# Six gathered tiles of a routed-expert kernel transposed by VectorE in quarter rows instead of by TensorE; joint gate inserts, a later table load, and another order of the last three units

## The chip, the cores and the metric

The kernel runs on one core of a Trainium2 chip. The metric is device time in microseconds, of the whole program, as the median of several executions. Besides, one execution was profiled; all rows below are from it. Its engines: TensorE (PE; PEld is its weight load), VectorE (DVE), ScalarE (ACT), GpSimd (POOL) and SyncE (SP), which issues plain DMAs in the order of its program. GpSimd issues the indirect DMAs (gathers and scatters).

## The reference

Three layers follow each other, all in float32:

```python
# 1. attention in chunks of 64: q, k, v are (4, 8, 576, 64)
scores = np.matmul(q_c, k_c.transpose(0, 1, 2, 4, 3)) / np.sqrt(D)
attn = softmax(scores)                  # per chunk
x = np.matmul(attn, v_c)                # -> (2304, 512)
# 2. dense layer: w_in (512, 2048), w_out (2048, 512)
h = x @ w_in
x = (h * np.clip(h + 3.0, 0.0, 6.0) / 6.0) @ w_out
# 3. routed experts: 8 experts, w1 (8, 512, 1024), w2 (8, 1024, 512)
noisy = x @ w_gate + np.log1p(np.exp(x @ w_noise)) * noise
top2 = the two largest of the 8 logits of each token
top2_w = softmax of these two
for e in range(8):
    for k in range(2):
        mask = top2[:, k] == e
        h = np.maximum(x[mask] @ w1[e], 0.0)
        out[mask] += top2_w[mask, k, None] * (h @ w2[e])
```

## The kernel before

Tokens are 18 tiles of 128. Every float32 matrix product is made from three passes (`PASSES`) of a high and a low part of each operand, so each tensor that TensorE reads is first split: ScalarE writes the high part, VectorE the low part.

The dense layer runs in five blocks of 4, 3, 4, 4 and 3 tiles; a block loops over 16 units of 128 hidden columns. In a unit TensorE computes the first layer (`mlp_s1`, L316, 12 matmuls), ScalarE and VectorE make the activation and its split (L357, L358, L362, L370), and TensorE adds the second layer of the unit before (`mlp_o`, L328, 3 matmuls for each tile). From the last block on, each unit also takes one unit of expert weights in (`pump`: L135 loads 512 KB, L141 and L142 split them); the raw loads have three buffers, and the load for three units ahead is issued behind L142.

The experts run in ten groups of rows: expert 0 in two (`(0, 0)` with 3 tiles, `(0, 1)` with 2), experts 1 to 6 in one of 5 tiles (608 rows), expert 7 in two again. A group loops over 8 units (`exp_h`: L316, L634, L635; `exp_o`: L328). Its rows come by a table: `gate_pos` gives every token a slot, and GpSimd writes the token's number and weight there (L557, two writes for a tile of tokens). `exp_slots` loads the table of a group (L568). Then there are two ways to bring rows in:

- `exp_gather` gathers whole rows of a tile by one indirect DMA (L609), and `exp_tr` transposes them by four TensorE transposes (L619), after which ScalarE and VectorE split them out of PSUM (L622, L623).
- `exp_slots_q`, `exp_index` and `exp_gather_q` make row numbers of quarter rows (L578, L580: SyncE; L586: VectorE), gather by four indirect DMAs for each tile (L592), and `exp_tr_q` transposes by VectorE in blocks of 32 x 32 (L407) and splits (L604, L605).

Before, groups (0, 0), (0, 1) and (1, 0) go the first way, all later ones the second. The order of TensorE, VectorE and ScalarE is the order of the program's text, from the last block on that of SyncE too; GpSimd's order is the scheduler's. Work put in between hangs on two clocks: `side`, a list run at the end of a unit, and `ticks`, run inside matmul sequences, where `tick()` counts 4 matmuls of a first layer or 3 of a second. `route` puts the gate of one block's tokens on ticks: `gate_t` transposes a tile (L431, L434), `gate_m` makes its logits (L447, L452), `gate_r` turns them back (L460, L469), `gate_top` picks two experts (L488 to L522, in four parts), and `gate_pos` (L534, L535 on TensorE, L550 to L557) gives the slots.

The gate of block 3 runs in block 4, that of block 4 in group (0, 0). At the end, `exp_last` does the last two units tile by tile, and `exp_y` scales a finished tile by its weights (L659, L661) and has GpSimd add it to the output (L662).

## Time and profile before

| what | us |
|---|---|
| median of 3 runs (lowest to highest) | 930.3 (928.49 to 930.64) |
| the profiled execution | 939.06 |
| its span, from the first to the last instruction | 937.2 |
| TensorE busy in the span | 909.9 (97%) |
| last MLP block and its gate | 388.8 to 471.6 |
| group (0, 0) | 471.6 to 513.8 |
| group (0, 1) | 513.8 to 536.6 |

A row of a timeline gives the start, the duration, the engine, the line, the operation with its tiles, and how many instructions were merged. A bracket at its end is the idle time of the engine before it and what ended it. SPq is SyncE issuing DMAs. TensorE's ends are modelled, so rows that follow each other overlap by some tenths: the distance from start to start is what counts.

### The profile page before, as it was taken

How to read it: one execution, taken by the hardware profiler on the slowest of the kernel's cores; microseconds unless marked ns; L12 is line 12 of the kernel's file. 1: busy time of each engine (PE TensorE's matmuls, PEld its weight loads, DVE VectorE, ACT ScalarE, POOL GpSimd, SP SyncE). 2: the span in 40 equal slices, each digit the busy share in tenths (PEclk: the TensorE clock that was granted, in tenths of full speed). 3: DMA queues.
4: the chain of work that ended last, by engine and by line, in shares of the span. 5: the costliest groups of instructions: out<-in, count | busy, mean ns of one | idle time of the engine just before them, and what ended most of it. 6: DMA issues, size and time to landing. Idle time of an engine off the chain costs nothing. (4 is left out here: it accounts for less than half of the span.)

```text
span 937.2 us, 14383 instructions
## 1 busy us (share of the span) xinstructions
PE 909.9 (97%) x5804; PEld 771.1 (82%) x5804; DVE 480.7 (51%) x908; ACT 330.7 (35%) x637; POOL 229.4 (24%) x213
## 2 busy tenths in 40 slices
PE   7999999999999999998999998999999999999996
PEld 4777788877778778877888887888898989888885
DVE  7999956545543553354552545444545444441311
ACT  4555633323322332243531533333433333321210
POOL 1000000030002000304005263663655445332311
PEclk9999999999999999999999998999999999999998
DMA  9736522121257400033532762563637355240422
GB/s 341 231 106 196 165 76 83 64 54 53 69 197 249 113 5 0 17 97 102 158 102 54 175 145 87 118 153 109 148 103 154 93 124 136 69 55 20 54 24 33
DMA packets 49916, 101.49 MB, mean 108 GB/s; under 512 B 17040, under 2 KB 23056, under 8 KB 49840
## 3 DMA queue, kind: packets, MB, share of 16 engines
q1 hardware_dynamic: 38736, 80.38, 27.4%
q0 software_dynamic: 11104, 20.10, 11.8%
q8 instruction: 47, 0.77, 0.4%
q14 instruction: 29, 0.24, 0.1%
HBM read 77.66 MB, written 22.75 MB: 107 GB/s over the span
## 5 line engine op out<-in xcount | busy, mean ns | idle before, releaser
L328 PE MATMUL bp<-w,g 128*128 128x512 f32 (+1 forms) x1812 | 454.5, 397 | 5.4 <-ACT g L362 3.2
L328 PEld LDWEIGHTS bp<-w,g 128*128 128x128 f32 (+1 forms) x1812 | 330.1, 186 | 81.5 <-ACT g L362 4.6
L316 PE MATMUL bp<-Xa,w 128*128 128x304 f32 (+3 forms) x1344 | 241.6, 330 | 2.9 <-ACT Xa L294 1.3
L316 PEld LDWEIGHTS bp<-Xa,w 128*128 128x128 f32 x1344 | 210.4, 189 | 26.3 <-issue 2.5
L557 POOL DMA_INDIRECT table<-pay,slot x36 | 36.0, 999 | 439.9 <-DVE slot L554 430.5
L592 POOL DMA_INDIRECT xrq<-x2d,iq x114 | 118.0, 1035 | 101.8 <-DVE iq L586 40.7
L635 DVE SCALAR_TENSOR_TENSOR g<-bp,g 128x304 fp32r<-128x304 f32 (+2 forms) x128 | 60.0, 472 | 144.2 <-ACT g L634 123.2
L142 DVE TENSOR_TENSOR w<-raw,w 128x1024 fp32r<-128x1024 f32 x64 | 78.5, 1226 | 90.1 <-ACT w L141 64.4
L634 ACT ACTIVATE g<-bp 128x304 fp32r<-128x304 f32 (+2 forms) x128 | 54.1, 425 | 181.0 <-PE bp L316 149.3
L316 PE MATMUL bp<-Xe,w 128*128 128x304 f32 (+1 forms) x672 | 106.4, 313 | 2.9 <-issue 2.7
L316 PEld LDWEIGHTS bp<-Xe,w 128*128 128x128 f32 x672 | 102.5, 192 | 7.3 <-issue 4.2
L316 PE MATMUL bp<-Xb,w 128*128 128x384 f32 (+1 forms) x480 | 106.3, 365 | 0.0
L316 PEld LDWEIGHTS bp<-Xb,w 128*128 128x128 f32 x480 | 86.1, 188 | 11.7 <-issue 1.0
L662 POOL DMA_INDIRECT out_dram<-arena,tab x40 | 63.1, 1577 | 125.6 <-DVE arena L659 102.2
L358 DVE SCALAR_TENSOR_TENSOR r<-r,bp 128x512 f32<-128x512 f32 (+1 forms) x80 | 50.6, 633 | 83.0 <-ACT r L357 73.6
L141 ACT ACTIVATE w<-raw 128x1024 fp32r<-128x1024 f32 x64 | 67.7, 1058 | 60.6 <-PE bp L328 42.6
L357 ACT ACTIVATE r<-bp,b 128x512 f32<-128x512 f32 (+1 forms) x80 | 51.3, 641 | 105.0 <-PE bp L316 102.2
L370 DVE TENSOR_TENSOR g<-r,g 128x512 fp32r<-128x512 f32 (+1 forms) x80 | 51.0, 637 | 39.7 <-ACT g L362 38.3
L362 ACT ACTIVATE g<-r 128x512 fp32r<-128x512 f32 (+1 forms) x80 | 47.3, 591 | 51.4 <-DVE r L358 47.2
L190 ACT ACTIVATE w<-u 128x512 fp32r<-128x512 f32 x32 | 20.3, 634 | 36.6 <-DVE u L177 33.9
L407 DVE STREAM_TRANSPOSE arena<-xrq 128x512 f32<-128x512 f32 (+1 forms) x30 | 31.3, 1044 | 0.0
L197 DVE TENSOR_TENSOR w<-u,w 128x512 fp32r<-128x512 f32 x32 | 22.0, 688 | 1.4
(152 smaller groups left out, 455.7 us busy)
## 6 DMA issues: line engine op xcount, KB each, us to landing
raw<-in_w2u_dram SPq DMA_DIRECT2D x64, 512.0 KB
raw<-in_w1u_dram SPq DMA_DIRECT2D x24, 512.0 KB
arena<-in_qkv_dram SPq DMA_DIRECT2D x14, 768.0 KB
out_dram<-zero SPq DMA_DIRECT2D x4, 1536.0 KB
rawx<-in_w1u_dram SPq DMA_DIRECT2D x8, 512.0 KB
x2d<-x SPq DMA_DIRECT2D x15, 256.0 KB
xq<-x2d SPq DMA_DIRECT2D x44, 64.0 KB
xrq<-x2d,iq POOLq DMA_INDIRECT x114
```

What stands on the lines that cost most here:

```text
L141: nc.scalar.activation(w[:, 0], raw, AF.Copy)
L142: nc.vector.tensor_tensor(w[:, 1], raw, w[:, 0].bitcast(F32), op=ALU.subtract)
L316: nc.tensor.matmul(dst, w[:, a, kd * P:(kd + 1) * P], x[:, b, kd, t0:t0 + n], start=(k == 0), stop=(k == 3 * KD - 1))
L328: nc.tensor.matmul(acc[i][:gi.shape[2]], gi[:, a], w[:, b, DM:], start=(first and j == 0), stop=(last and j == 2))
L357: nc.scalar.activation(r, st["h", b], AF.Relu, bias=b3)
L358: nc.vector.scalar_tensor_tensor(r, r, 6.0, st["h", b], op0=ALU.min, op1=ALU.mult)
L362: nc.scalar.activation(st["g", b, u][:, 0], st["r", b], AF.Copy)
L370: nc.vector.tensor_tensor(g[:, 1], st["r", b], g[:, 0].bitcast(F32), op=ALU.subtract)
L592: nc.gpsimd.indirect_dma_start(out=xr[:, c * P:(c + 1) * P], out_offset=None, in_=x2q, in_offset=bass.IndirectOffsetOnAxis(ap=st["iq", key ...
L634: nc.scalar.activation(g[:, 0, t0:t0 + n], h, AF.Relu)
L635: nc.vector.scalar_tensor_tensor(g[:, 1, t0:t0 + n], h, 0.0, g[:, 0, t0:t0 + n].bitcast(F32), op0=ALU.max, op1=ALU.subtract)
L662: s = nc.gpsimd.indirect_dma_start(out=out, out_offset=bass.IndirectOffsetOnAxis(ap=tab[:n, i, 0:1], axis=0), in_=y, in_offset=None, compu ...
```

## The change

Five things are changed.

- Groups (0, 0) and tiles 0 to 2 of group (1, 0) are brought in by quarter rows: `exp_slots_q`, `exp_index`, `exp_gather_q` and `exp_tr_q` take the place of `exp_slots`, `exp_gather` and `exp_tr`. For group (0, 0) the turns move from units 11 to 13 to units 12 to 14. Tiles 3 and 4 of group (1, 0) keep the first way, but their transposes move to units 1 and 2 of group (0, 1), and the others come in units 3, 5 and 6; indices and first gathers are put ahead of the second layer that ends group (0, 0).
- `route` handles two tiles (of four) or three (of three) at once: transposes of all, then one `gate_m`, one `gate_r`, with a third tile `at2` for the copies. `gate_top` has other ticks, and `gate_pos` moves from tick 26 to 24 in block 4 and from 17 to 13 in group (0, 0).
- In block 4 the table is loaded 18 ticks after `gate_pos`, and index and gathers follow 12 ticks later; in group (0, 0) they stay with `gate_pos`.
- `exp_last` does the last three units tile by tile (the second layer of unit 5 is left out of its old place); the activation of unit 7 has its own buffer.
- The last tile's scaling is split in halves between VectorE and ScalarE.

```diff
--- before.py
+++ after.py
@@ -95,7 +95,7 @@
     early = const.tile([P, NE], F32, name="early")
     quarter = const.tile([P, 1], F32, name="quarter")
     wg_sb = const.tile([P, KD, 32], F32, name="wg_sb")
-    lp = const.tile([P, 2 * P], F32, name="lp")
+    lp = const.tile([P, 3 * P], F32, name="lp")
     noise_sb = const.tile([P, NTILE, NE], F32, name="noise_sb")
     pay = const.tile([P, NTILE, 2, 2], I32, name="pay")
     cnt = const.tile([P, NE + 1], I32, name="cnt")
@@ -431,14 +431,15 @@
             nc.tensor.transpose(pt[:, kd, :], x, ident)
 
     def gate_cp(t, i=1):
-        nc.scalar.activation(at_[i], st.pop(("x2p", t)), AF.Copy)
-        st["x2T", t] = at_[i].rearrange("p b (c j) -> p b c j", c=KD)
+        x = at_[i] if i < 2 else work.tile([P, KD, P], F32, tag="r", bufs=2, name="at2")
+        nc.scalar.activation(x, st.pop(("x2p", t)), AF.Copy)
+        st["x2T", t] = x.rearrange("p b (c j) -> p b c j", c=KD)
 
     ENDS = [pairs[0][:, :2 * P], pairs[0][:, 6 * P:]]
 
-    def gate_m(t, tag="p6"):
-        gate_mm([t], bank(tag, [P, P], "lg"))
-        gate_lp([t])
+    def gate_m(ts, tag):
+        gate_mm(ts, bank(tag, [P, DM], "lg"))
+        gate_lp(ts)
 
     def gate_mm(ts, lg):
         for i, t in enumerate(ts):
@@ -451,9 +452,9 @@
     def gate_lp(ts):
         nc.scalar.activation(lp[:, :len(ts) * P], st.pop(("lg", ts[0])), AF.Copy)
 
-    def gate_r(t, tag="p6"):
-        gate_rt([t], bank(tag, [P, P], "lt"))
-        gate_rr([t])
+    def gate_r(ts, tag):
+        gate_rt(ts, bank(tag, [P, DM], "lt"))
+        gate_rr(ts)
 
     def gate_rt(ts, lt):
         for i in range(len(ts)):
@@ -586,11 +587,11 @@
         nc.vector.tensor_scalar(iq[:, :tq.shape[1]], tq, float(KD), quarter, op0=ALU.mult, op1=ALU.add)
         st["iq", key] = iq
 
-    def exp_gather_q(key, i):
+    def exp_gather_q(key, i, rows=NROW):
         xr = work.tile([P, DM], F32, tag="x2", bufs=3, name="xrq")
         for c in range(min(P, st["xg", key].shape[3] - i * P) // 32):
             nc.gpsimd.indirect_dma_start(
-                out=xr[:, c * P:(c + 1) * P], out_offset=None, in_=x2q,
+                out=xr[:, c * P:(c + 1) * P], out_offset=None, in_=x2q[:rows * KD],
                 in_offset=bass.IndirectOffsetOnAxis(ap=st["iq", key][:, i * KD + c:i * KD + c + 1], axis=0))
         st["xr", key, i] = xr
 
@@ -625,8 +626,11 @@
     def exp_h(key, e, u, nt):
         x, w = st["xg", key], st["w", e, u]
         n = x.shape[3]
-        g = gtile()[:, :2 * n].rearrange("p (j n) -> p j n", j=2)
-        st["g", key, u] = g
+        if (key, u) == ((NE - 1, 1), U2 - 1):
+            g = work.tile([P, DM], F32R, tag="r", bufs=2, name="gl")
+        else:
+            g = gtile()
+        g = st["g", key, u] = g[:, :2 * n].rearrange("p (j n) -> p j n", j=2)
         parts = [(0, n)] if n <= DM else [(0, n // 2), (n // 2, n // 2)]
         for t0, n in parts:
             h = hbank(n)
@@ -637,7 +641,7 @@
 
     def exp_last(key, e, nt):
         for i in range(nt):
-            for u in (U2 - 2, U2 - 1):
+            for u in range(U2 - 3, U2):
                 g, w = tile_of(st["g", key, u], i), st["w", e, u]
                 for j, (a, b) in enumerate(PASSES):
                     nc.tensor.matmul(st["acc", key][i][:g.shape[2]], g[:, a], w[:, b, DM:],
@@ -655,7 +659,10 @@
             n = min(P, rows - i * P)
             y, acc = arena[:n, i], st["acc", key][i][:n]
             sc = tab[:n, i, 1:2].bitcast(F32)
-            if i % 2 == 0 or key == (NE - 1, 1):
+            if (key, i) == ((NE - 1, 1), nt - 1):
+                nc.vector.tensor_scalar(y[:, :DM // 2], acc[:, :DM // 2], sc, None, op0=ALU.mult)
+                nc.scalar.activation(y[:, DM // 2:], acc[:, DM // 2:], AF.Copy, scale=sc)
+            elif i % 2 == 0 or key == (NE - 1, 1):
                 nc.vector.tensor_scalar(y, acc, sc, None, op0=ALU.mult)
             else:
                 nc.scalar.activation(y, acc, AF.Copy, scale=sc)
@@ -818,7 +825,7 @@
         for f, *a in lst:
             f(*a)
 
-    EU = 11
+    EU = 12
     prev = []
 
 
@@ -981,22 +988,28 @@
 
     groups += [((NE - 1, 0), NE - 1, 0, 3, ("b", 0)), ((NE - 1, 1), NE - 1, 3, CT - 3, ("a", 0))]
 
-    def route(g, grp, rows, n0=17, late=0):
+    def route(g, grp, rows, n0=13, late=0, settle=0):
 
         t, nt = GRP[g]
-        steps = []
-        for i in range(nt):
-            steps += [(5 + 2 * i, gate_r, t + i, "p" + "76"[i % 2]), (3 + 2 * i, gate_m, t + i, "p" + "76"[i % 2]),
-                      (2 if i == 1 else 1 + 2 * i, gate_t, t + i, "p6" if i == 1 else "p5", i % 2)]
-        steps.sort(key=lambda x: (x[0], (gate_r, gate_t, gate_m).index(x[1])))
-        steps = [(n + late, *a) for n, *a in steps]
-        last = 3 + 2 * nt + late
-        d = (n0 - last) // 4
+        steps, n = [], late
+        for k in (3,) if nt == 3 else (2, 2):
+            ts = list(range(t, t + k))
+            steps += [(n + 1 + i, gate_t, t + i, ("p5", "p6", "p7")[i], i) for i in range(k)]
+            steps += [(n + k + 2, gate_m, ts, "p5" if k == 3 else "p7"), (n + k + 4, gate_r, ts, "p6" if k == 3 else "p7")]
+            t, n = t + k, n + k + 3
+        last = n + 2
+        d = max((n0 - last) // 4, 1)
         steps += [(last + i * d, gate_top, g, 1) for i in range(4)]
         if g == len(GRP) - 1:
             steps += [(last, gate_base, g)]
-        steps += [(n0, gate_pos, g), (n0, exp_slots, *grp)]
-        steps += [(n0, exp_gather, grp[0], i, rows) for i in range(grp[3])]
+        steps.sort(key=lambda x: x[0])
+        steps += [(n0, gate_pos, g)]
+        if settle:
+            steps += [(n0 + settle, exp_slots_q, *grp), (n0 + settle + 12, exp_index, grp[0])]
+            steps += [(n0 + settle + 12, exp_gather_q, grp[0], i, rows) for i in range(grp[3])]
+        else:
+            steps += [(n0, exp_slots, *grp)]
+            steps += [(n0, exp_gather, grp[0], i, rows) for i in range(grp[3])]
         for n, f, *a in steps:
             at(ticks, st["tick"] + n, f, *a)
 
@@ -1016,9 +1029,9 @@
     order = tc.manual_schedule(engines={nc.tensor.engine, nc.vector.engine, nc.scalar.engine, nc.sync.engine})
     order.__enter__()
     side = {}
-    at(side, 0, route, len(GRP) - 2, groups[0], NROW - BT[NB - 1] * P, 26, 3)
+    at(side, 0, route, len(GRP) - 2, groups[0], NROW - BT[NB - 1] * P, 24, 3, 18)
     for i in range(3):
-        at(side, EU + i, exp_tr, (0, 0), i)
+        at(side, EU + i, exp_tr_q, (0, 0), i)
     regular(NB - 1, side)
 
 
@@ -1029,10 +1042,12 @@
         if gi == 0:
             at(side, 5, counts)
         elif gi == 1:
-            at(side, 0, exp_slots, *nxt_)
-            for i in range(nxt_[3]):
-                at(side, i, exp_gather, nxt_[0], i)
-                at(side, min(3 + i, 7), exp_tr, nxt_[0], i)
+            for i in (3, 4):
+                at(side, i - 2, exp_tr, nxt_[0], i)
+            for i in range(3):
+                if i:
+                    at(side, i, exp_gather_q, nxt_[0], i)
+                at(side, (3, 5, 6)[i], exp_tr_q, nxt_[0], i)
             at(side, 4, exp_slots_q, *after)
         elif gi == 2:
             at(side, 0, exp_index, nxt_[0])
@@ -1061,6 +1076,11 @@
                     at(side, (3, 5, 6)[i], exp_gather_q, after[0], i)
         for u in range(U2):
             if (gi, u) == (1, 0):
+                exp_slots_q(*nxt_)
+                exp_index(nxt_[0])
+                for i in (3, 4):
+                    exp_gather(nxt_[0], i)
+                exp_gather_q(nxt_[0], 0)
                 exp_o(prevg[0], prevg[1], U2 - 1, prevg[2])
                 exp_y(*prevg)
             exp_h(key, e, u, nt)
@@ -1071,7 +1091,8 @@
                 exp_last(key, e, nt)
                 st["most"] = nc.values_load(cnt[0:1, NE:], min_val=0, max_val=RGN)
             elif u > 0:
-                exp_o(key, e, u - 1, nt)
+                if (gi, u) != (len(groups) - 1, U2 - 2):
+                    exp_o(key, e, u - 1, nt)
             elif prevg is None:
                 for b, v in prev:
                     mlp_o(b, v)
```

## Rows read from the trace of the kernel before

**Rows 1.** First part of the page: busy time and share of each engine.

```profile
PE 909.9 (97%) x5804; PEld 771.1 (82%) x5804; DVE 480.7 (51%) x908; ACT 330.7 (35%) x637; POOL 229.4 (24%) x213
```

**Rows 2.** Timeline around the first wait of TensorE.

```profile
436.90 0.38 SPq L568 DMA_DIRECT2D tab<-table  x1
...
441.98 1.06 ACT L141 ACTIVATE w<-raw 128x1024 fp32r<-128x1024 f32 x1 [6.03 <-DMA raw<-in_w2u_dram]
...
445.37 3.91 PE L328 MATMUL bp<-w,g 128*128 128x512 f32 x9 [2.87 <-ACT g L362]
```

**Rows 3.** Stretches: length, PE busy (matmuls), granted clock, DMA share, GB/s.

```profile
445.40:449.10 3.70, 3.70 (x9) 0.54 0.94 269
...
510.54:514.00 3.46, 3.46 (x19) 1.00 0.64 182
```

**Rows 4.** Chain of waits, group (0, 1): start, us, what.

```profile
522.14 1.41 PE bp L328 x6
523.55 0.47 PE bp L619 x4
524.01 1.33 PE bp L316 x12
```

**Rows 5.** Timeline of TensorE at its second wait.

```profile
510.54 0.75 PE L619 MATMUL bp<-ident,xr 128*128 128x128 f32 x4 [1.23 <-DMA xr<-x2d,tab]
```

**Rows 6.** Timeline of TensorE at its third wait.

```profile
562.41 0.46 PE L328 MATMUL bp<-w,g 128*96 128x512 f32 x1 [0.57 <-issue]
...
565.60 7.14 PE L316 MATMUL bp<-Xe,w 128*128 128x304 f32 x24 [2.74 <-issue]
```

**Rows 7.** Timeline of units of the last MLP block.

```profile
427.67 2.26 PE L316 MATMUL bp<-Xa,w 128*128 128x384 f32 x12
...
431.86 2.25 PE L316 MATMUL bp<-Xa,w 128*128 128x384 f32 x12
...
460.61 2.27 PE L328 MATMUL bp<-w,g 128*128 128x512 f32 x9
...
460.87 0.58 ACT L357 ACTIVATE r<-bp,b 128x384 f32<-128x384 f32 x1 [1.09 <-PE bp L316]
...
462.08 0.53 ACT L362 ACTIVATE g<-r 128x384 fp32r<-128x384 f32 x1 [0.62 <-DVE r L358]
...
462.92 1.06 ACT L141 ACTIVATE w<-raw 128x1024 fp32r<-128x1024 f32 x1 [0.32 <-PE bp L328]
...
464.01 1.23 DVE L142 TENSOR_TENSOR w<-raw,w 128x1024 fp32r<-128x1024 f32 x1 [0.82 <-ACT w L141]
```

**Rows 8.** Timeline of SyncE, table and row numbers in group (0, 1).

```profile
527.26 0.43 SPq L568 DMA_DIRECT2D tab<-table  x1
...
532.39 1.88 SPq L580 DMA_DIRECT2D tq<-tq  x3
```

**Rows 9.** DMA traffic, 40 slices of 0.1 us from 558.5.

```profile
GB/s 0 41 0 0 0 0 0 0 0 82 246 82 164 41 41 0 0 0 0 0 0 0 246 123 246 41 0 0 0 164 164 0 0 287 41 123 205 246 328 369
```

**Rows 10.** Timeline of the end.

```profile
927.81 1.56 POOL L662 DMA_INDIRECT out_dram<-arena,tab  x1 [15.26 <-DVE arena L659]
...
929.68 1.43 POOL L662 DMA_INDIRECT out_dram<-arena,tab  x1 [0.31 <-issue]
```

**Rows 11.** Timeline of the gate in group (0, 0).

```profile
485.42 0.27 PE L460 MATMUL bp<-ident,lp 128*128 128x128 f32 x1
...
490.11 0.56 DVE L510 TENSOR_TENSOR macc<-macc,m 128x8 bf16<-128x8 bf16 x3
```

**Rows 12.** Timeline of one tile turned by VectorE in group (1, 0).

```profile
569.70 1.10 DVE L407 STREAM_TRANSPOSE arena<-xrq 128x512 f32<-128x512 f32 x1
...
571.49 0.69 DVE L605 TENSOR_TENSOR Xa<-arena,Xa 128x512 fp32r<-128x512 f32 x1 [0.70 <-ACT Xa L604]
```

**Rows 13.** Timeline of GpSimd.

```profile
516.26 1.57 POOL L662 DMA_INDIRECT out_dram<-arena,tab  x1 [0.30 <-DVE g L635]
...
559.08 0.94 POOL L592 DMA_INDIRECT xrq<-x2d,iq  x1 [0.30 <-issue]
```

## The prediction

> **What bounds the kernel now.** First the share of each engine on the page: TensorE is busy for 97% of the span [rows 1], so time can be won only by taking work from it or by closing its gaps. So the next view is TensorE's line of the timeline from the last MLP block to the first full expert group (390 to 580 us), looking for an idle time in brackets. There are three. In the first [rows 2] TensorE waits 2.87 us for L362. Read upward, ScalarE had stood 6.03 us before L141, a weight split, for its raw weights: SyncE issues in order, and the load of the table (L568) stood before the raw loads until the eight table writes had landed, and went at 436.90. The granted clock of the stretch behind it is 0.54 [rows 3], the lower level (1.2 GHz), and its nine second-layer matmuls fill 3.7 us, where the chain of waits has 1.40 for six [rows 4], so 2.1 for nine: 1.6 us more. Price of the first wait: 4.5 us. The second [rows 5] is 1.23 us for the gather of expert 0's second part; the stretch behind it is granted 1.00, the upper level (2.4 GHz) [rows 3]. The third [rows 6] has no releaser but "issue": 0.57 us inside one run of matmuls and 2.74 behind it, and the next 24 matmuls take 7.14 us, where 304 columns at the rate of [rows 4] (12 x 224 in 1.33) make 3.6. That is 6.8 us together, and I know no instruction behind it.
>
> The profiled execution took 939.06, the median is 930.3. Without the third gap it would be 932.3, so I take that gap as belonging to this execution alone, and sum what both have in common.
>
> **Gains.** (1) Six tiles lose four TensorE transposes each; the chain has 0.47 us for four [rows 4]: 6 x 0.47 = 2.8.
>
> (2) The first wait. A `tick` is 4 first-layer or 3 second-layer matmuls; in the last block a unit is 4.19 us (427.67 to 431.86) [rows 7] and 6 ticks, so a tick is 0.70 us. `gate_pos` goes from tick 26 to 24 and so in VectorE's order ahead of one L370 and one L142 (some 0.6, and 1.23): the table writes begin 1.4 + 1.8 - 0.6 (a wait, below) = 2.6 us earlier, and the table can be loaded at 434.3. Its load now stands at tick 42, behind three more raw loads, which no longer wait. Behind it SyncE has more to do than before: the row numbers (L578), and three copies of them (L580) that wait until they land. In a later group that was 5.1 us from the table load to the first copy, and 1.9 for the copies [rows 8]: free at 441.3, 3.9 later than before (437.4). The raw load that stands behind it is due three units (12.6 us) later than the one that stood there before, so it is 8.7 us less late; I leave 1 us of that for VectorE, which is less behind in that unit than it was. The 6.0 us that ScalarE waited are covered with 1.7 to spare. `exp_index`, at tick 54 (431.86 + 12 x 0.70 + 0.6 = 440.9), waits on VectorE for the copies: the last is issued at 440.7, and lands by 442.2 to 442.9 (an estimate; a small gather takes 2.2 [rows 9]). Queued behind it are L370 and L142; L370 ends at 443.0 to 443.7 and is wanted at 443.5. So the whole 4.5 is won. Bounds: 0 and 4.5.
>
> (3) The gather of expert 0's second part: `gate_pos` 4 ticks earlier (2.8 us, less 0.5 for a wait, below) moves writes, table and gather forward by more than 1.23: 1.2 won; bounds 0 and 1.2.
>
> (4) The end. The first of the two last tiles is now complete nine matmuls (2.1 us) before the last, not six, and the last tile's scaling is halved between two engines. GpSimd's two output writes start at 927.81 and 929.68 [rows 10], the second because the first is in front of it. The first moves forward by three matmuls, 0.7 us, and the second with it to 929.0; its data, by a scaling of half the length, are ready no later (an estimate): 0.7 won; bounds 0.3 and 1.0. TensorE's own work stays, in another order.
>
> Sum of gains: 2.8 + 4.5 + 1.2 + 0.7 = 9.2.
>
> **Losses.** (a) TensorE waits in `gate_pm` for the sums in `macc`. In expert 0 the chain from the last tile's transpose (485.42) to the last `macc` addition (490.67) is 5.25 us [rows 11]; the program has 8 ticks for it (5.6 us), now 6, with two of the three transposes more in front: 4.6 us against about 5.1, a wait of 0.5. In the last block VectorE has a fourth tile and L142, L358, L370 between the parts, some 7.6 us by the same rows, and 10 ticks are 7.0: 0.6. Sum 1.1; bounds 0 and 1.3. Fewer and larger copies are on ScalarE, hidden.
>
> (b) The first three turned tiles, in units 12, 13 and 14. Count from the end of the first layer of unit 12. In the undisturbed unit [rows 7] that is 460.61; L357 starts 0.26 later, L362 ends 1.74 after L357's start, and L141 to the end of L142 is 2.32, over at 4.63. Now the turn follows: L407, L604 on ScalarE, L605, one behind the other, 2.48 us from 569.70 to 572.18 [rows 12], L604 over 0.7 before the end. L604 stands ahead of the next L357 in ScalarE's order, and L605 ahead of L358 in VectorE's. Tile 0: L604 until 6.4, so unit 13's L362 ends at 8.1, just before TensorE wants it at 8.4. Its L141 and L142 are over at 10.4, tile 1's L604 at 12.2, unit 14's L362 at 13.9, wanted at 12.6: TensorE waits 1.3. L142 is over at 16.2, tile 2's turn at 18.6. TensorE comes to the first matmul of group (0, 0), which reads all three tiles, at 14.7 without a wait: with 0.2 for its first pass it loses 3.7 in all. With no backlog from tiles 0 and 1 (L142 over at 13.0) it would still be 13.0 + 2.5 - 14.7, less the first pass: 0.6. Bounds 0.6 and 3.7; I take 3.7, since the order on both engines is fixed by the program.
>
> (c) The three of expert 1. GpSimd now has twelve quarter gathers where it had three, in a group of eight units of 1.40 + 1.33 us [rows 4]. Count from the group's first matmul. The index is ready 0.8 before it (behind the first L623: 510.54, and some 2.3 for transposes, L622, L623 and L586; the group begins 0.47 + 0.47 + 2.1 behind 510.54). Quarter gathers follow each other at 0.95 + 0.30, output writes at 1.57 + 0.30 [rows 13]: tile 0 until 4.2 to 4.4, three output writes until 10.0, tile 1 until 15.0, tile 2 until 20.0. The last is issued at 18.75 and lands 2.2 later, as the one issued at 559.08 is seen on the DMA line until 561.1 [rows 9]; with the turn 23.4. TensorE is due at 8 x 2.73 + 2 x 0.47 - 1.40 = 21.4, so it waits 2.0, and for the PSUM bank behind it, whose L634 and L635 stand behind the turn, 0.6 more: 2.6. Bounds: with the two later tiles gathered ahead of the output writes, only the turns hold it: 1.1; with the output writes ahead of all twelve, 3.8.
>
> (d) The clock behind these two waits of some 2.2 us. Behind 1.23 us nothing [rows 3, 5], behind 2.87 us 1.6 [rows 2, 3]; between them in proportion 1.0 each: 2.0; bounds 0 and 3.2.
>
> Losses: 1.1 + 3.7 + 2.6 + 2.0 = 9.4. Net 0.2 lost: **930.5** as a median, and 932.5 in a profiled execution without the third gap.
>
> The later table order, indices and raw loads of group 2 on have the same lines in the same units, and are taken as unchanged.
>
> **The rivals.** *Forecast*: what is won in the table wait is given back at the two turns, 927 to 933: 44%.
>
> *The turns hide* (faster): the backlog of (b) is absorbed and GpSimd gathers ahead of the output writes, 9.2 - 1.1 - 0.6 - 1.1 = 6.4, so 923.9. For it: VectorE is busy half of the span [rows 1], and from the group of expert 2 on the same turn runs without a wait; against it: a unit there has two first-layer halves and five tiles, here the units are 4.2 and 2.7 us. 30%.
>
> *The table still holds SyncE* (slower): one mechanism, the row-number copies. If SyncE is free after 443, the raw load is later than its cover, and VectorE stands at `exp_index`: the first wait stays, 930.5 + 4.5 = 935.0. It decides at 1.7 us more than I give the chain. 14%.
>
> *The turn is dearer in full* (slower or same): output writes first and the lower clock behind both waits: 9.2 - 1.1 - 3.7 - 3.8 - 3.2 = -2.6, so 932.9. A rule of the Trainium skill speaks for this direction: "VectorE: DVE Perf Modes", section "Rules for kernel authors", names TensorE for a full 128 x 128 turn wherever the result may lie in PSUM, which here it may. By that rule the move is a loss. The trace agrees in the price of one tile (0.47 us against 2.48) but not in whose time counts, since TensorE is the full engine. 12%.
>
> **The numbers.** A measurement of this kernel tells 0.3% (2.8 us) from no change: 927.5 to 933.1. Faster: the second case, 30, and 6 of the forecast's: 0.36. Slower: 14, 6 of the last case, 4 of the forecast's: 0.24. Same: 0.40. All bounds at their good end give 922.5, at their bad end 939.1; 923.5 to 935.5 leaves out some 2 in 10.
>
> **What the profile after would show.** (2) right: no bracket on TensorE between 440 and 446, L141 there without a DMA wait. (a): short waits of L534 or L535 on DVE. (b): a gap before the first L316 on Xb of group (0, 0), released by L604 or L605. (c): a gap before the first L316 on Xe, and L592 in one unbroken row on GpSimd before it. No gap at (b) and (c) makes the forecast wrong by 6 us; a gap at unit 9 or 10 with L141 or L586 waiting makes it wrong on the other side.

## The result, and the profile after

The changed kernel takes 936.93 us (median of five runs, 935.11 to 938.84) against 930.3: ratio 1.0074, 95% interval 1.0056 to 1.0092. It is 6.6 us slower where 930.5 was forecast, and outside the range. Its profiled execution took 935.11 us, with a span of 932.9 and a mean granted clock of 0.993; its other four runs have 0.989 to 0.991. So the profile shows its mildest run, without the third gap of [rows 6].

First part of the page after (busy time, share of the span, instructions), beside [rows 1]:

```profile
PE 904.0 (97%) x5780; PEld 767.2 (82%) x5780; DVE 486.6 (52%) x912; ACT 331.4 (36%) x634; POOL 251.6 (27%) x231
```

Timelines of SyncE, VectorE, TensorE and ScalarE after, where [rows 2] showed the first wait:

```profile
436.60 0.38 SPq L569 DMA_DIRECT2D tab<-table  x1
437.03 0.48 SPq L579 DMA_DIRECT2D tq<-table  x1
439.16 1.87 SPq L581 DMA_DIRECT2D tq<-tq  x3
...
442.30 0.23 DVE L587 TENSOR_SCALAR iq<-tq,quarter 128x12 int32<-128x12 int32 x1 [4.62 <-DMA tq<-tq]
...
443.05 1.90 PE L328 MATMUL bp<-w,g 128*128 128x512 f32 x7 [1.97 <-DVE g L370]
...
445.06 1.05 ACT L141 ACTIVATE w<-raw 128x1024 fp32r<-128x1024 f32 x1
```

L141 no longer stands before its raw weights, so the wait that was to go is gone. But VectorE stands at `exp_index` (L587) until 442.30, L370 is behind it, and TensorE loses 1.97 us. The table load went at 436.60, 7.2 us behind the start of the last of the eight table writes; in the kernel before it went 2.7 us behind it. Two raw loads, which before came only behind the table load, now stand ahead of it and run beside the writes (SyncE and GpSimd, after and then before):

```profile
424.53 0.33 SPq L135 DMA_DIRECT2D raw<-in_w2u_dram  x1
428.32 0.33 SPq L135 DMA_DIRECT2D raw<-in_w2u_dram  x1
429.44 0.96 POOL L558 DMA_INDIRECT table<-pay,slot  x1 [0.30 <-issue]
```

```profile
423.31 0.33 SPq L135 DMA_DIRECT2D raw<-in_w2u_dram  x1
434.24 0.98 POOL L557 DMA_INDIRECT table<-pay,slot  x1 [0.30 <-issue]
```

Timelines of TensorE and ScalarE after, at the end of the last MLP block (tiles of group (0, 0)):

```profile
464.79 2.49 PE L328 MATMUL bp<-w,g 128*128 128x512 f32 x9 [0.96 <-ACT g L362]
468.65 0.45 PE L316 MATMUL bp<-Xb,w 128*128 128x384 f32 x1 [1.37 <-ACT Xb L605]
...
467.97 0.63 ACT L605 ACTIVATE Xb<-arena 128x512 fp32r<-128x512 f32 x1 [2.28 <-DVE arena L407]
```

Timelines of GpSimd, VectorE, ScalarE and TensorE after, in group (0, 1) (tiles of expert 1):

```profile
513.04 0.95 POOL L593 DMA_INDIRECT xrq<-x2d,iq  x1 [0.30 <-issue]
514.29 1.66 POOL L669 DMA_INDIRECT out_dram<-arena,tab  x1 [0.30 <-issue]
516.25 2.23 POOL L669 DMA_INDIRECT out_dram<-arena,tab  x1 [0.30 <-issue]
518.79 1.55 POOL L669 DMA_INDIRECT out_dram<-arena,tab  x1 [0.30 <-DVE Xe L624]
520.65 1.01 POOL L593 DMA_INDIRECT xrq<-x2d,iq  x1 [0.31 <-issue]
...
525.43 1.12 POOL L593 DMA_INDIRECT xrq<-x2d,iq  x1 [0.30 <-issue]
...
530.19 1.08 DVE L407 STREAM_TRANSPOSE arena<-xrq 128x512 f32<-128x512 f32 x1 [4.15 <-DMA xrq<-x2d,iq]
...
531.31 0.63 ACT L605 ACTIVATE Xe<-arena 128x512 fp32r<-128x512 f32 x1 [6.66 <-DVE arena L407]
...
533.18 0.74 PE L328 MATMUL bp<-w,g 128*128 128x512 f32 x2 [3.26 <-ACT g L638]
534.50 2.07 PE L328 MATMUL bp<-w,g 128*128 128x512 f32 x4 [0.58 <-DVE g L639]
536.37 5.85 PE L316 MATMUL bp<-Xe,w 128*128 128x304 f32 x24
```

Read from the bottom: TensorE waits for L638 of unit 6; ScalarE had L605 of the second turned tile ahead of it; VectorE waited 4.15 us for that tile's rows; GpSimd issued the last of its four gathers at 525.43, behind three output writes. The stretches behind the waits (length, busy times, granted clock, DMA share, GB/s):

```profile
443.00:445.20 2.20, 2.15 (x10) 1.83 (x11) 1.61 (x3) 0.57 (x2) 1.47 (x1) 1.00 0.97 389
464.80:471.40 6.60, 4.95 (x21) 3.73 (x22) 4.53 (x7) 3.46 (x5) 0.00 (x0) 1.00 0.26 79
534.20:541.00 6.80, 6.43 (x21) 5.39 (x22) 5.00 (x7) 3.19 (x5) 0.00 (x0) 0.50 0.63 183
```

Behind the first two the clock stays at the upper level; behind the third it is at the lower one (1.2 GHz) for 6.8 us, which costs about half of them, 3.4.

### The profile page after: what moved, and what is told of

Read it like the earlier page. It is cut to its first block, busy times and chain, and to the rows that moved or that the text cites. A ratio compares the mean times of both kernels' runs of the same rounds, so it can differ in the third digit from the quotient of the medians.

```text
span 932.9 us, 14375 instructions
## 1 busy us (share of the span) xinstructions
PE 904.0 (97%) x5780; PEld 767.2 (82%) x5780; DVE 486.6 (52%) x912; ACT 331.4 (36%) x634; POOL 251.6 (27%) x231
## 4 chain that ended last, share of the span: by engine, by line
PE 47%; DMA 2%; DVE 2%; POOL 1%; issue 1%; ACT 1%; SPq 0%; POOLq 0%; DVEq 0%; ACTq 0%
PE bp L328 23%; PE bp L316 23%; DMA table<-pay,slot 1%; DVE arena L407 1%; DMA xrq<-x2d,iq 0%; ACT w L141 0%; POOL table L558 0%; POOL xrq L593 0%; POOL out_dram L669 0%; DMA tq<-table 0%; PE bp L647 0%; DVE Xb L606 0%; ACT Xb L605 0%; PE bp L620 0%; DMA tq<-tq 0%
## 5 line engine op out<-in xcount | busy, mean ns | idle before, releaser
L316 PE MATMUL bp<-Xa,w 128*128 128x304 f32 (+3 forms) x1344 | 240.3, 330 | 2.1 <-ACT Xa L294 1.3
L316 PEld LDWEIGHTS bp<-Xa,w 128*128 128x128 f32 x1344 | 210.4, 188 | 25.4 <-ACT Xa L294 1.4
L593 POOL DMA_INDIRECT xrq<-x2d,iq x138 | 145.6, 1055 | 115.6 <-issue 49.7
L638 ACT ACTIVATE g<-bp 128x304 fp32r<-128x304 f32 (+2 forms) x127 | 53.9, 424 | 169.9 <-PE bp L316 169.8
L316 PE MATMUL bp<-Xb,w 128*128 128x384 f32 (+1 forms) x480 | 107.0, 366 | 1.6 <-ACT Xb L605 1.4
L316 PEld LDWEIGHTS bp<-Xe,w 128*128 128x128 f32 x672 | 102.2, 192 | 4.0 <-DVE Xe L606 0.4
L316 PE MATMUL bp<-Xe,w 128*128 128x304 f32 (+1 forms) x672 | 105.1, 312 | 0.1
L316 PEld LDWEIGHTS bp<-Xb,w 128*128 128x128 f32 x480 | 86.0, 188 | 14.0 <-ACT Xb L605 1.8
L141 ACT ACTIVATE w<-raw 128x1024 fp32r<-128x1024 f32 x64 | 67.7, 1058 | 55.2 <-PE bp L328 55.2
L370 DVE TENSOR_TENSOR g<-r,g 128x512 fp32r<-128x512 f32 (+1 forms) x80 | 51.0, 637 | 39.6 <-ACT g L362 39.5
L407 DVE STREAM_TRANSPOSE arena<-xrq 128x512 f32<-128x512 f32 (+1 forms) x36 | 37.9, 1053 | 4.2 <-DMA xrq<-x2d,iq 4.2
```

Source lines behind the costliest of these rows:

```text
L141: nc.scalar.activation(w[:, 0], raw, AF.Copy)
L316: nc.tensor.matmul(dst, w[:, a, kd * P:(kd + 1) * P], x[:, b, kd, t0:t0 + n], start=(k == 0), stop=(k == 3 * KD - 1))
L370: nc.vector.tensor_tensor(g[:, 1], st["r", b], g[:, 0].bitcast(F32), op=ALU.subtract)
L407: nc.vector.transpose(dst.rearrange("p (c b j) -> p c b j", c=c, b=KD), src.rearrange("p (c i b) -> p c b i", c=c, b=KD))
L593: nc.gpsimd.indirect_dma_start(out=xr[:, c * P:(c + 1) * P], out_offset=None, in_=x2q[:rows * KD], in_offset=bass.IndirectOffsetOnAxis(ap= ...
L638: nc.scalar.activation(g[:, 0, t0:t0 + n], h, AF.Relu)
```

## The experiments

Every kernel was timed beside the kernel before on the same chip. The chips differ: on two of them the kernel before takes 928.7 to 928.8 us, on three others 937.9 to 939.9. The turned tiles of group (0, 0) (`Xb` in the rows) are called "(0, 0) tiles", those of group (1, 0) (`Xe`) "expert 1's tiles". The last column is the kernel's own median.

| kernel | ratio to before, 95% interval | before there | us |
|---|---|---|---|
| `no_bc` | 0.9943 [0.993, 0.9956] | 928.72 | 922.98 |
| `no_b` | 1.0019 [1.001, 1.0027] | 928.72 | 929.99 |
| `no_c` | 1.0008 [0.9999, 1.0017] | 928.72 | 928.82 |
| `only_bc` | 1.0073 [1.0057, 1.0089] | 928.72 | 934.83 |
| `only_table` | 0.9965 [0.9951, 0.9979] | 928.8 | 925.17 |
| `b_index` | 0.9989 [0.998, 0.9998] | 928.8 | 928.43 |
| `b_split` | 0.9974 [0.9964, 0.9984] | 928.8 | 926.02 |
| `c_early` | 1.0011 [1.0002, 1.002] | 928.8 | 929.57 |
| `table_gate` | 0.9937 [0.9922, 0.9952] | 938.08 | 932.1 |
| `pad10` | 0.9944 [0.9928, 0.9959] | 938.08 | 932.6 |
| `c_last` | 1.0011 [0.9999, 1.0023] | 938.08 | 939.31 |
| `both` | 1.0019 [1.0004, 1.0033] | 938.08 | 939.39 |
| `no_bc_2` | 0.9931 [0.9908, 0.9953] | 939.87 | 932.83 |
| `c_one` | 0.9968 [0.9955, 0.9982] | 939.87 | 936.49 |
| `c_last_2` | 1.0014 [0.9998, 1.003] | 939.87 | 940.71 |
| `both_2` | 1.0027 [1.0009, 1.0045] | 939.87 | 942.81 |
| `c_last_3` | 1.0021 [1.0001, 1.0042] | 937.94 | 939.22 |
| `both_3` | 1.0017 [0.9995, 1.0039] | 937.94 | 939.51 |

**Which part loses.** The turned tiles were undone in one group, in the other, in both, or kept alone.

```diff
-            steps += [(n0 + settle, exp_slots_q, *grp), (n0 + settle + 12, exp_index, grp[0])]
-            steps += [(n0 + settle + 12, exp_gather_q, grp[0], i, rows) for i in range(grp[3])]
+            steps += [(n0 + settle, exp_slots, *grp)]
+            steps += [(n0 + settle, exp_gather, grp[0], i, rows) for i in range(grp[3])]
...
-        at(side, EU + i, exp_tr_q, (0, 0), i)
+        at(side, EU + i, exp_tr, (0, 0), i)
```

That is `no_b`, which undoes the (0, 0) tiles. `no_c` undoes expert 1's: the branch `gi == 1` and the five lines ahead of the second layer that ends group (0, 0) have the text of the kernel before. `no_bc` does both; `only_bc` keeps the turned tiles and the later table load, and gives `route`'s gates and the end the text of the kernel before.

> The changed kernel with the three tiles of group (0,0) gathered as whole rows and turned by TensorE again, everything else of the change kept (the row table of that group is still loaded 18 ticks later). Theory T1 (the change loses by the new waits around its VectorE turns and by the half clock behind them): the wait for `exp_index` (1.97 us) and the three waits at the turned tiles (0.96, 1.37 and 0.28 us) go, and three rows of four transposes come back (some 1.4 us), so about 3 us less than the changed kernel: near 934, ratio to the kernel before near 1.004. Rival R1 (only the GpSimd row of gathers for expert 1 costs anything): within 1 us of the changed kernel, ratio near 1.007.

> The changed kernel with the five tiles of expert 1's first group gathered as whole rows and turned by TensorE again, everything else of the change kept. T1: the two waits at 533 to 535 us (3.26 and 0.58 us) go, and with them the half-clock stretch of 6.8 us behind them (some 3.4 us); three rows of transposes come back (1.4 us): about 6 us less than the changed kernel, near 931, ratio near 1.001. Rival R2 (the gates in one insert, or the later table load, cost the time): within 1 us of the changed kernel.

> The changed kernel with all six tiles turned by TensorE again: what is left of the change is the gates in one insert, the row table of group (0,0) loaded later, and the last three units tile by tile. T1: the losses all sit at the turned tiles, so this is faster than the kernel before: 926 to 928, ratio 0.996 to 0.998. Rival R2 (the gates or the later load cost the time): no faster than the kernel before, ratio 1.003 or more.

> The kernel before with the six turned tiles alone (quarter rows, VectorE), with the row table of group (0,0) loaded at the changed kernel's tick; gates tile by tile and the end as in the kernel before. T1: the whole loss and some more, since what the gates and the end win is gone: 937 to 939, ratio 1.007 to 1.010. Rival R2: near the kernel before, ratio 1.000 to 1.003.

`no_bc` beats both kernels: 5.7 us under the one before, more than T1 gave. TensorE has no idle time in its stretches (columns as above):

```profile
440.00:470.00 30.00, 30.00 (x156) 27.16 (x155) 17.98 (x24) 16.10 (x25) 3.67 (x3) 1.00 0.49 151
505.00:545.00 40.00, 40.00 (x262) 36.18 (x261) 22.59 (x34) 17.79 (x30) 16.13 (x14) 1.00 0.73 170
```

Beside it the (0, 0) tiles cost 5.8 us (`no_c`) and expert 1's 7.0 (`no_b`). R1 and R2 fall: both groups lose, the rest of the change wins. The parts don't add up to the last us: `only_bc` stands 6.1 over the kernel before, where 5.8 + 7.0 less the 3.6 of the table load (`only_table`, by its medians) make 9.2.

**What the rest wins.** `only_table` is the kernel before with the table load of group (0, 0), and the gathers behind it, at `n0 + 16`; `table_gate` is `no_bc` with the old end.

> The kernel before with the row table of group (0,0) loaded 16 ticks later, and its whole-row gathers behind it; nothing else of the change. If the gain of `no_bc` is that of the first wait, as the forecast has it (4.5 us): ratio 0.995 to 0.996. If the gates in one insert and the end carry it: 0.998 to 1.000.

> `no_bc` without the changes at the end (two last units tile by tile, one scaling of the last tile): what is left is the later table and the gates in one insert. By the forecast's terms the end is worth 0.7 us and the gates cost 1.1 against a gather wait of 1.2: ratio 0.995 to 0.996 by these. If the end is worth nothing beside the longer end in `no_bc`: 0.994.

The later load wins 0.35% (3.3 us of 930.3; 4.5 forecast). `table_gate`, on another chip, stands with `no_bc` and `no_bc_2`: the new end wins nothing that shows, the gates 0.2 to 0.3%.

**The (0, 0) tiles.** `b_index` is `no_c` with `settle + 15` in place of `settle + 12`; `b_split` also takes L605 and L606 of the first two tiles out of the turn:

```diff
-        at(side, EU + i, exp_tr_q, (0, 0), i)
-    regular(NB - 1, side)
+        at(side, EU + i, exp_tr_q, (0, 0), i, i < 2)
+    A = {}
+    for i in range(2):
+        at(A, EU + i + 1, exp_hl_q, (0, 0), i)
+    regular(NB - 1, side, A)
```

> The variant `no_c` (tiles of group (0,0) in quarter rows, expert 1 by TensorE) with `exp_index` and the gathers behind it given out 3 ticks later, so that VectorE reaches `exp_index` after L370 and L142 of that unit instead of ahead of L370. Theory T2 (the early place of `exp_index` on VectorE costs 1.97 us and is one part of what the quarter rows of group (0,0) lose): some 2 us under `no_c`, ratio near 0.9985, and no wait of TensorE for `g` of L370. Rival R3 (the wait is only moved: the turns come later by as much): no better than `no_c`, ratio 1.000 or more.

> `b_index`, and the split of the first two turned tiles (L605, L606) given out behind L362 of the next unit instead of ahead of its L357 and L358; the third tile as in the changed kernel. T2 (the rest of the loss comes from L357 and L358 standing behind the split): the waits of 0.96, 1.37 and 0.28 us shrink to under 0.5 together, the tiles now cost nothing beside what their transposes cost: at or under `no_bc`, ratio 0.992 to 0.995. Rival R3 (DMA traffic of the quarter rows or VectorE's time as such): no better than `b_index`.

`b_index` wins 0.19% over `no_c` (1.8 us, on two chips of the same sort), and TensorE no longer waits for L370. The wait that it removes differs from run to run: 1.97 us in the changed kernel, 1.90 in `only_bc`, but 0.43 in the profiled execution of `no_c`, whose table load went earlier (435.23). So the 1.8 us stand on the medians, not on that trace. `b_split` wins 0.15% more; of the three waits at the tiles one stays, split in two (TensorE, `b_split`):

```profile
465.14 0.44 PE L316 MATMUL bp<-Xb,w 128*128 128x384 f32 x1 [0.90 <-ACT Xb L612]
465.87 2.21 PE L316 MATMUL bp<-Xb,w 128*128 128x384 f32 x11 [0.28 <-DVE Xb L613]
```

T2 holds for both places, as far as waits go. Still `b_split` is 0.3% over `no_bc`, more than expected. Its last output write is only 0.76 us later than that of `no_bc` (GpSimd, `no_bc` and then `b_split`); the spans are 921.6 and 924.2:

```profile
913.45 1.43 POOL L669 DMA_INDIRECT out_dram<-arena,tab  x1 [0.75 <-ACT arena L664]
```

```profile
914.21 1.43 POOL L676 DMA_INDIRECT out_dram<-arena,tab  x1 [0.76 <-ACT arena L671]
```

So 1.8 us are lost behind the last write, from its end to the end of the span: 921.6 - 914.88 = 6.7 us in `no_bc`, 8.6 in `b_split`, and 8.3 and 8.0 in `no_c` and `no_b`. What these three share is GpSimd's count on the page, 222 for 213. `pad10` is `no_bc` with ten idle instructions:

```diff
-        nc.gpsimd.memset(tmpi[:, :, 1], 0)
+        z = nc.gpsimd.memset(tmpi[:, :, 1], 0)
+        with tc.issue_after(z.ins):
+            for i in range(10):
+                nc.gpsimd.memset(pad[:, i:i + 1], 0.0)
```

> `no_bc` with ten one-column memsets more on GpSimd, far ahead of the change (beside the constants at the kernel's start), where GpSimd has nothing to do. Theory T4 (the end, from the last output write to the last instruction, 6.1 us in the kernel before, 6.7 in `no_bc` and 8.3 to 8.5 in `no_c` and `b_split`, hangs on the number of GpSimd instructions in the program, 329 and 339): the end goes from 6.7 to about 8.4 us, ratio near 0.996. Rival R5 (the end hangs on what the DMA queues still have to do, or on chance): no change, 0.994.

Its last write and span (930.2):

```profile
920.69 1.43 POOL L670 DMA_INDIRECT out_dram<-arena,tab  x1 [0.75 <-ACT arena L665]
```

8.1 us, against 6.7 and 6.8 in the two traces of `no_bc`, and all eight traces with a count of 222 have 8.0 to 8.7. That speaks for T4, but doesn't show it: with 213 the five traces have 6.1 to 7.4 (7.4 in `table_gate`, on `pad10`'s own chip), with 216 the one trace (`c_one`) 6.4, and with 231 the five 6.8 to 7.4. So the time doesn't grow with the count, and the ratio, 0.9944, can't tell 1.4 us from none.

**Expert 1's tiles.** `c_early` and `c_last` are `no_b` with the three output writes issued behind the second and the third tile's gathers:

```diff
+    def exp_held():
+        with tc.issue_after(st["last_q"].ins):
+            for a in st.pop("held"):
+                exp_w(*a)
...
+                if i == 1:
+                    at(side, 1, exp_held)
...
-                exp_y(*prevg)
+                exp_y(*prevg, hold=True)
```

(`i == 2`, `side` 2 in `c_last`.) `both` is the changed kernel with `c_last`'s order and `b_split`'s places.

> The variant `no_b` (group (0,0) by TensorE, three tiles of expert 1 in quarter rows) with GpSimd issuing the four gathers of the second of these tiles ahead of the three output writes of group (0,0) instead of behind them. The number of instructions and of bytes stays. T3 (the second tile lands at 530 us because its gathers stand behind three writes, and its split holds L638): the tile lands some 6 us earlier, the waits of 3.26 and 0.58 us and the half clock behind them go, ratio at or under that of `no_bc`, 0.992 to 0.995. Rival R4 (quarter rows are slow to land, or VectorE is short of time in these units): ratio stays at 1.000 or more.

> `c_early` with the three output writes behind the gathers of the third quarter-row tile as well. In `c_early` the second tile was in time, and the wait moved to the third (2.81 and 0.25 us ahead of the first L316 on `Xe`, then half clock). T3 (what the tiles of expert 1 lose is GpSimd's order: any tile behind the writes is late): no wait of TensorE at these tiles, no half clock behind them, 3 to 4 us under `c_early`, ratio 0.993 to 0.998. Rival R4 (VectorE is short of time in these units, whatever the order): 1.000 or more.

> The changed kernel with all three mends: `exp_index` of group (0,0) 3 ticks later, the split of its first two tiles behind L362, the output writes of that group behind the gathers of expert 1's three tiles. T1 to T3 (the loss is in these three places): 12 us of the changed kernel's time go but for the longer end and a rest at the third tile of (0,0): ratio 0.993 to 0.998. Rival (part of the loss is in the quarter rows as such): above 1.000.

In `c_early` the wait of 3.26 is gone and another is there, for the third tile, now the only one behind the writes (TensorE):

```profile
529.67 0.48 PE L316 MATMUL bp<-Xe,w 128*128 128x304 f32 x1 [2.81 <-ACT Xe L605]
```

With 0.25 us behind it, the lower clock for 3.4 us (1.7 lost) and less 1.4 of transposes, this wait makes 3.4 of the 3.6 us by which the last write is later than that of `no_bc` (917.02 against 913.45), so a late tile is what `c_early` loses ahead of the last write. In `c_last` 0.5 and 0.3 us are left of the wait, and no trace of `c_last` or `both` has the lower clock there. Yet T3's number failed: `c_last` and `both` stay over the kernel before. Where the waits had been won, ScalarE now starts late on a matmul that had long ended (ScalarE, `c_last`; TensorE's L316 for this L638 ended at 513.0):

```profile
516.69 0.36 ACT L638 ACTIVATE g<-bp 128x224 fp32r<-128x224 f32 x1 [3.42 <-PE bp L316]
518.19 0.49 ACT L623 ACTIVATE Xe<-bp 128x384 fp32r<-128x384 f32 x1 [1.14 <-remote]
```

The repeats were to tell the program from the chip:

> `c_last` once more, to tell two causes apart. If the 4.1 us at 513 to 518 us belong to the program (eight and more gathers in a row on GpSimd ahead of the raw weights), they are there again and the ratio stays at 1.000 to 1.002. If they belong to that chip or run: gone, ratio 0.995 to 0.998.

> `both` once more. As for `c_last_2`: the stall again and 1.001 to 1.003, or gone and 0.994 to 0.998.

> `no_b` with one quarter-row tile of expert 1 instead of three: the first, whose gathers stand ahead of the output writes; the second and third as whole rows (one gather each) by TensorE. T3 (the loss is the eight gathers behind the writes): no wait at these tiles, no stall before them, ratio 0.994 to 0.996. Rival R4 (each quarter-row tile costs some 2.3 us by itself, a third of what the three cost): 0.997 or more.

> `no_bc` once more, as the level for the three beside it: 0.993 to 0.996 again, if the gain of the later table load and the gates doesn't hang on the chip.

> `c_last` a third time. On a chip where the kernel before takes 928 to 930 us: by T3 no wait at the turned tiles, no late start of ScalarE, ratio 0.995 to 0.997 (level of `no_bc` less 1.4 us of transposes, plus some 1.7 us for the longer end and what is left of the waits); by R4 1.000 or more. On a chip where it takes 938 or more: 1.000 to 1.002 again.

> `both` a third time. Where the kernel before takes 928 to 930 us: by T1 to T3 0.994 to 0.997; by R4 1.000 or more. Where it takes 938 or more: 1.001 to 1.003 again.

All came to chips where the kernel before takes 938 to 940. There `no_bc` wins 0.7%, `c_last` and `both` come out at 1.001 to 1.003 again, and one tile (`c_one`: only the first of the three in quarter rows) costs about half of that difference. Its ratio, 0.9968, lies between what T3 said (up to 0.996) and what R4 said (0.997 and more), and its interval holds both; T3's numbers for three tiles are missed in all six runs of `c_last` and `both`, so R4 has the better of it on these chips. ScalarE's idle time before this eviction was 3.4 us in `c_last`, `both` and `both_3`, 0.7 at the next one in `c_last_2`, and none in `both_2` and `c_last_3`; the eviction of a tile turned by TensorE starts 0.8 us late in `c_last_2`, and in `c_one` (ScalarE; TensorE's transposes ended at 511.5):

```profile
512.37 0.60 ACT L623 ACTIVATE Xe<-bp 128x512 fp32r<-128x512 f32 x1 [2.33 <-PE bp L620]
```

`no_bc_2` has nothing of the kind there. What holds ScalarE isn't in the traces, and it isn't there in every execution. Whether `c_last` wins where the kernel before takes 929 was not seen: no run of it came to such a chip.

## Why the prediction was wrong

**Right.** What is neither turn nor its index came to 5.3 us (0.57%), where 4.5 + 1.2 + 0.7 - 1.1 = 5.3 were forecast. That the sum is met is luck: the table load won 3.3 for 4.5, the rest 2.0 for 0.8, though the new end, 0.7 of that, wins nothing that shows. The gather wait of [rows 5] is gone, and of the 1.1 at the gates 0.4 came. The transposes won are in the counts of both pages: 24 matmuls less. The places of (b) and (c) were named, with their releasers.

**Failed: (2), that `exp_index` loses nothing.** The step that failed is the time from the table writes to the table load. The sum moved the load forward by what the writes gained, as if they would land as soon as before. Counted from the first layer ahead of the wait (438.36; in the forecast 440.25 and 0.6 for a wait of the gate, 440.9), the writes begin where they were forecast, 18.8 us ahead (19.1). But the load came 7.16 us behind the start of the last write, not 2.66: by that count 4.8 us later than forecast. In the traces of all 18 runs of the variants, which have the load at the later place, it came 3.9 to 6.2 us behind. That the raw loads beside the writes (two, where the sum had three ahead of the load) cause this is read from these times and not tested by itself. The copies behind the load took 4.4 us to their end where 7.0 were forecast, so the index was some 2 us late: L587 ran at 442.30, and TensorE lost 1.97. `b_index` won it back. This is the rival "the table still holds SyncE" by half: the index chain was late, but the raw loads behind it were not, so the price was 2.0 and not 4.5.

**Right in place and nearly in size: (b).** The brackets at the tiles add up to 2.6 us for 3.7; from start to start it is 3.4, since the changed kernel's matmuls are 0.8 us behind those of `no_bc` ahead of the tiles and 4.2 behind them (by the same count `exp_index` costs 2.1). In `no_c`'s own trace 3.4 here and 0.6 at `exp_index`, less 1.4 of transposes, make 2.6. Its last write is 3.2 later than that of `no_bc` (916.67, 913.45), of which 0.5 lie ahead of both places; 3.3 was forecast, with 1.0 for the clock. The other 1.6 of the span's 4.8 come behind the last write, which no term had.

**Failed: (c), by its size and its tile.** The forecast took only the last tile as late, 2.6 us. It was the second: three writes took 6.4 us from the first's start to the next gather, not 5.6, four gathers 5.9 for 5.0, and the last landed 4.6 us behind its start (chain of waits), not 2.2. So VectorE had it at 530.19, and L638 of unit 6 stood behind its L605: 3.84. And that longer wait brought the lower clock for 6.8 us, 3.4 lost where (d) gave 1.0 in proportion. In `no_b`'s own trace the wait is 3.21, again with 6.8 us at the lower clock (527.80 to 534.50 has 0.50): 3.21 + 3.4 - 1.4 is 5.2, and 5.4 is what the last write shows (918.83 against 913.45). The medians have 7.0, of which 1.3 come behind the last write; forecast were 2.2. Wait and clock stand at or just over their upper bounds, 3.8 and 3.2, where the sum had taken the middle.

**Failed: (d), the clock in proportion to the wait.** In the changed kernel's profile two waits of 2 us (1.97, and 2.6 in three parts) brought nothing and one of 3.26 + 0.58 brought 6.8 us. But the same waits do other things in other executions: in `only_bc` 1.90 us at L370, then 0.96 + 1.37 + 0.29 at the tiles, then 3.01 at expert 1's, and in `b_index` 1.02 + 1.36 + 0.29, were each followed by 3.4 us at the lower clock (stretches within these, `only_bc` and then `b_index`):

```profile
444.10:447.50 3.40, 3.40 (x12) 3.10 (x11) 1.82 (x3) 1.58 (x2) 2.79 (x3) 0.50 0.93 333
471.45:474.80 3.35, 3.35 (x12) 3.26 (x11) 1.79 (x2) 1.71 (x3) 0.00 (x0) 0.50 0.00 0
536.30:539.60 3.30, 3.13 (x7) 1.75 (x7) 2.60 (x4) 0.95 (x3) 0.00 (x0) 0.50 0.80 215
```

```profile
467.50:470.88 3.38, 3.38 (x11) 3.38 (x12) 2.06 (x3) 1.47 (x2) 0.00 (x0) 0.50 0.08 30
```

In `no_c` the same three waits at the tiles were followed by none. So a wait of some 2 us cost nothing more, or 1.7 us, and not 1.0. The medians show the same: the changed kernel's runs have mostly 0.991, those of the kernel before, on the chips where it takes 929, mostly 0.995, `no_bc` 0.997. 0.004 of 930 us at half clock is 7.4 us long and costs 3.7 (an estimate from the mean clocks; the end of the span, at the lower clock in both traces, is in them, with 6.2 us in the changed kernel and 6.8 in the one before), over half of the 6.6. The term had the two waits' 2.0 less the 1.6 won at the first wait. The profiled run is the mildest because three of the other four have 0.002 less, which is one more such stretch (1.7 us, an estimate).

**The sum.** 2.1 at `exp_index`, 1.2 at (c) (3.84 for 2.6) and 3.1 at (d) (3.4, and 1.7 for the median run, for 2.0) are 6.4, the whole of 936.93 - 930.5. The errors of the other terms cancel, which is luck. (All bounds at their bad end add up to 939.2, not 939.1.) Of the rivals, "the turn is dearer in full" (932.9) had (c) and (d) at about the size that the profile shows; the wait at `exp_index` it hadn't. Its 2.48 us for a tile has the splits L604 and L605 in it, which the way by TensorE needs too (L622, L623); the turn alone is 1.10 [rows 12].

**Not settled.** What the quarter rows of expert 1 cost once GpSimd's order is mended, and why ScalarE starts late there. On those chips the third gap differs as well from trace to trace (4.3 us of waits with 3.4 at the lower clock in `pad10`, 5.1 with 6.8 in `c_last`, on the same chip), so two traces don't part the tiles from it. Also open is what fills the time behind the last write. The version to keep is `no_bc`: 0.9943, and 0.9931 on another chip.

## What to carry to other kernels

Work taken from the full engine pays only if what takes it over has room at that place: here 0.47 us of TensorE were exchanged for a chain over GpSimd, DMA, VectorE and ScalarE, and each place where that chain stood ahead of an instruction TensorE waits for cost more than the transposes. For a tile that comes by many small gathers, count every queue that it stands in to the landing, and check every tile against its own due time, not only the last. A load that is moved behind others runs beside their traffic: the time that its chain took in the old place is no price for the new one. Cost a wait with the clock behind it, as something that may or may not come, and test the parts of a change one by one: the best version here is the change without its main part.

## What the runs showed of the hardware

The time behind the last output write was 6.1 to 8.7 us; with ten idle GpSimd instructions far ahead it was 8.1, where the same kernel without them had 6.7 and 6.8 (`table_gate`, with as few of them as that kernel, had 7.4). Behind waits of 1.9 to 2.0 us, and of 2.6 us in three parts, the granted clock stayed at the upper level in some executions (the changed kernel, `no_c`) and fell to the lower one for 3.4 us in others (`only_bc`, `b_index`); behind single waits of 2.8 to 3.3 us it fell in all five traces that have one ahead of the third gap, for 3.4 or 6.8 us. The load that waits for the eight table writes came 2.7 us behind the start of the last one with no raw load beside the writes, and 3.9 to 7.2 us with raw loads beside them. On three chips the same kernel took 1% longer than on two others, and there TensorE waits again where [rows 6] shows the third gap (TensorE, `no_bc_2`, at the same unit):

```profile
560.38 0.44 PE L316 MATMUL bp<-Xe,w 128*128 128x304 f32 x2 [1.54 <-issue]
563.52 3.41 PE L316 MATMUL bp<-Xe,w 128*128 128x304 f32 x12 [2.70 <-DVE g L639]
```

All ten traces from these chips show it, and none of the nine of kernels other than the one before from elsewhere. So that gap belongs to some chips rather than to one execution, against what the prediction took it for; leaving it out of the sum was right, since the median of 930.3 is without it. On one of these chips one of 23 executions of the kernel before took 929.52, so it isn't there in each.
